# Triangular inverses in a delta-rule attention kernel: 16-by-16 blocks on VectorE, joined to 32-by-32 by TensorE

## The chip, the cores and the metric

The kernel runs on one core of one Trainium2 chip. The metric is the device time of one execution in microseconds (us), from the first to the last instruction with what lies around them; lower is better. The median of three runs of the kernel before is 1263.36 us.

## What is computed

A delta-rule attention over 4 batches, 8 heads, 768 tokens and a head dimension of 48 is followed by two dense feed-forward stages on 3072 tokens of 384 features. The reference, cut to what matters:

```python
def _attn_ref(q, k, v, beta):
    k_n = k / (np.linalg.norm(k, axis=-1, keepdims=True) + 1e-06)
    for t in range(S):
        kt, vt, bt = (k_n[:, :, t], v[:, :, t], beta[:, :, t, None])
        y[:, :, t] = np.einsum('bhd,bhde->bhe', q[:, :, t], state)
        v_old = np.einsum('bhde,bhd->bhe', state, kt)
        state = state + bt[:, :, :, None] * np.einsum('bhd,bhe->bhde', kt, vt - v_old)

def _moe_ref(x, w_in, w_out):            # 384 -> 2048 -> 384
    h = np.maximum(x @ w_in, 0.0)
    return (h * h @ w_out)

def _moe2_ref(x, w_gate, w_val, w_out):  # 384 -> 1536 -> 384
    gate = 1.0 / (1.0 + np.exp(-(x @ w_gate)))
    return (gate * (x @ w_val) @ w_out)
```

## The kernel before

**Attention by chunks.** The 768 tokens are cut into 12 chunks of 64. Inside a chunk the recurrence is solved at once: a strictly triangular 64-by-64 matrix A (k k^T times a factor for each row, tile `am`) gives the inverse of I + A, and the rest of the chunk is products with it. A unit is a pair of heads of one batch in one chunk; its head a = 0 lies on partitions 0 to 63, a = 1 on 64 to 127. A group g is two chunks, which is 32 units in four pieces j of 8; there are six groups.

**The inverse.** Of each 64-by-64 matrix the two diagonal 32-by-32 blocks are inverted by VectorE (DVE) in `invert_ops`: three transposes bring A into `xi` with one instance of a block on each partition, then `row(j)` for j = 31 down to 1 subtracts multiples of row j in `tt` (a multiply on L408 and a subtract on L415; columns in two spans, 0 to 21 and 22 to 31, where both exist), then `t_out` (L420) and `t_1` (L425) transpose back into `t64` and `t1` (which is the place of `xi`). The block between the two is made by TensorE (PE) and ScalarE (ACT): `n_piece` (L440) multiplies A's block with the one inverse, `w_piece` (L460) with the other, four pieces to a group. `t_piece`, `y_piece`, `s_piece` and `ks_piece` then use `t64`.

**The two stages.** In the first stage six passes, one for each group, run 16 iterations of the first feed-forward (`moe1_h`, L603, and `moe1_o`, L642), with weights as pairs of 12-bit parts, three products for each product of the reference. ACT squares, DVE or GpSimd (POOL) makes the low part `gl` (L628), and POOL the low parts of the weights (`ol`, `il`, L130). The attention of the next groups is spread over these passes. In the second stage (from about 800 us) only the second feed-forward is left (L849, L879).

**What sets the order.** Every engine's instructions are issued in the order in which the program writes them. Before the first pass the order is a list written by hand, `P_['start']`, in which `('d', n)` puts n products that nothing reads (`keep_warm`, L717, 512 columns each) on PE, and `('inv', w)` lets DVE take steps of an inverse of a weight w. In the passes each half of an iteration is a slot, 32 to a pass, and a table gives every piece the slot at which it is written. The steps of an inverse are in the queue `t_ops`; `invert_by` takes as many at each slot as it needs to be done at the slot `t_due`. The conversion of the raw weights (`narrow`: ACT L147, DVE L152 to L165, POOL L172) is spread over the start and the first pass.

The lines on which the change bears:

```python
tmp = [atc.tile([128, n], F32, name=f"tmp{n}") for n in (128, 224)]
spans = [(i, max(j, lo), hi) for i, (lo, hi) in enumerate(((0, CUT), (CUT, 32))) if hi > j]
ops += [(0.3 + 0.0021 * j * (32 - j), lambda j=j: row(j)) for j in range(31, 0, -1)]
ops += [(1.2, lambda: t_out(32)), (1.2, t_1)]
ops += [(1.2, lambda q=q: t_out(0, slice(32 * q, 32 * q + 32))) for q in (0, 2)]
```

Of the kernel before, what the change touches and what calls it, by code (L numbers as in the profile page):

```python
# [27 lines left out]
P_ = {'start': [('kn', 0, 1), ('kc', 0, 0), ('d', 1), ('kn', 0, 0), ('kn', 0, 2), ('kn', 0, 3), ('kc', 0, 1),  # L28
# [72 lines left out]
def kernel(  # L101
# [86 lines left out]
    # The last four blocks' places hold raw weights until it is their turn.  # L188
# [57 lines left out]
    tmp = [atc.tile([128, n], F32, name=f"tmp{n}") for n in (128, 224)]  # L246
# [4 lines left out]
    # What y's contraction takes from both sides, head a and b: tokens' rows at 0 and 64 (U; the  # L251
    # masked k q^T), d's at 64 and 0 (S; q^T).
# [68 lines left out]
    def norms(g):  # L321
        """beta / (|k| + 1e-6) and +-beta / (|k| + 1e-6)^2; one Newton step after Sqrt."""
# [45 lines left out]
    def scores_p(g, j):  # L368
        """k q^T where the token of k is the earlier one."""
# [17 lines left out]

    def invert_ops():
        """The inverses' 32 x 32 diagonal blocks: 128 instances (32 rows of a head, unit) on the
        partitions, xi [column, row], tt [column, row] of the transpose."""  # L390
# [6 lines left out]
        def t_in2(q):  # L397
            P = slice(32 * q, 32 * q + 32)
            nc.vector.transpose(out=xi[P], in_=am[P, :, 32:64].rearrange("p u c -> p c u"))

        def row(j):
            # Two spans of the columns, which do not depend on each other.
            spans = [(i, max(j, lo), hi) for i, (lo, hi) in enumerate(((0, CUT), (CUT, 32))) if hi > j]
            tv = {}
            for i, lo, hi in spans:
                n = hi - lo
                tv[i] = tmp[i][:, 0:j * n].rearrange("p (c i) -> p c i", i=n)
                nc.vector.tensor_tensor(  # L408
                    out=tv[i],
                    in0=xi[:, 0:j, j].unsqueeze(2).to_broadcast([128, j, n]),  # L410
                    in1=tt[:, j, lo:hi].unsqueeze(1).to_broadcast([128, j, n]),
                    op=ALU.mult,
                )
            for i, lo, hi in spans:
                nc.vector.tensor_tensor(  # L415
                    out=tt[:, 0:j, lo:hi], in0=tt[:, 0:j, lo:hi], in1=tv[i], op=ALU.subtract
                )
# [8 lines left out]

        ops = [(1.2, t_in), (1.2, lambda: t_in2(1)), (1.2, lambda: t_in2(3))]
        ops += [(0.3 + 0.0021 * j * (32 - j), lambda j=j: row(j)) for j in range(31, 0, -1)]
        ops += [(1.2, lambda: t_out(32)), (1.2, t_1)]
        ops += [(1.2, lambda q=q: t_out(0, slice(32 * q, 32 * q + 32))) for q in (0, 2)]  # L430
        return ops

# [62 lines left out]
    def t_piece(g, j):  # L495
        R = kv_t[g, j][:, :, HD:2 * HD]
# [31 lines left out]
    def y_piece(g, j):  # L528
# [104 lines left out]
    def moe1_o(n):  # L633
# [76 lines left out]
    def keep_warm(n, out=None):  # L710
        """Products that nothing reads, which keep the array's clock up while it waits."""
# [7 lines left out]
    with tc.manual_schedule():  # L719
# [15 lines left out]
        for g in range(1, NG):  # L735
            put_chain(g, S1 * (g - 1) + base[g])
            if g + 1 < NG:
                put_scores(g + 1, S1 * (g - 1) + base[g], S1 * g + base[g + 1])
# [4 lines left out]
        # The places of the raw weights of f, and who has them next.  # L743
        nxt = {f: f + 3 for f in range(NF1 - 7)}
        nxt.update({NF1 - 6: NF1 - 4, NF1 - 5: NF1 - 3, NF1 - 3: NF1 - 2, NF1 - 2: NF1 - 1})
        for f, t in zip(range(4, NF1), P_["cv"]):
# [165 lines left out]
def _layout(inputs):  # L912
# [8 lines left out]
    # axes: half, b2, pair, head, step, token, d  # L921
# [43 lines left out]
```

## Time and profile before

| | |
|---|---|
| runs | 1255.98, 1263.36, 1266.18 us |
| span of the profiled execution | 1259.9 us |
| busy PE, DVE, ACT, POOL | 1131.8, 749.4, 532.0, 392.3 us |
| start, until the first product of the first feed-forward | 0 to 97 us |
| first stage, first pass (17 iterations until the next pass's first `moe1_o`) | 97 to 286 us |
| second, third and fourth pass | 286 to 406, 406 to 532, 532 to 665 us |
| fifth and sixth pass | 665 to 740, 740 to 800 us |
| second stage | 800 to 1260 us |

The shares of busy time are means over stages with different limits, so the table cuts the span where a pass's `moe1_o` begins. PE counts a product in single precision (the attention's) as two instructions. The granted clock of PE has two levels, 1.2 and 2.4 GHz, shown as 0.50 and 1.00; a value between is a mean over a stretch.

### The profile page before, as it was taken

How to read it: one execution, taken by the hardware profiler on the slowest of the kernel's cores; microseconds unless marked ns; L12 is line 12 of the kernel's file. 1: busy time of each engine (PE TensorE's matmuls, PEld its weight loads, DVE VectorE, ACT ScalarE, POOL GpSimd, SP SyncE). 2: the span in 40 equal slices, each digit the busy share in tenths (PEclk: the TensorE clock that was granted, in tenths of full speed). 3: DMA queues.
4: the chain of work that ended last, by engine and by line, in shares of the span. 5: the costliest groups of instructions: out<-in, count | busy, mean ns of one | idle time of the engine just before them, and what ended most of it. 6: DMA issues, size and time to landing. Idle time of an engine off the chain costs nothing.

```text
span 1259.9 us, 24397 instructions
## 1 busy us (share of the span) xinstructions
PE 1131.8 (90%) x10040; PEld 923.1 (73%) x10040; DVE 749.4 (59%) x1416; ACT 532.0 (42%) x998; POOL 392.3 (31%) x331
## 2 busy tenths in 40 slices
PE   7675568789978997798899999999999999999997
PEld 4354456668856775586678888788888888888886
DVE  7999999996899599969954323342222222222222
ACT  3144354546544654465347668532122222222211
POOL 3444474644354345433333555200010100001000
PEclk9677679988989999899869999999999999999999
DMA  9014422602234224512313012320101010010101
GB/s 246 9 66 143 120 93 73 188 18 87 82 119 118 89 80 126 151 59 82 108 39 115 26 63 82 107 75 3 48 1 51 1 45 6 1 51 1 26 1 26
DMA packets 59552, 88.98 MB, mean 71 GB/s; under 512 B 31536, under 2 KB 39344, under 8 KB 59440
## 3 DMA queue, kind: packets, MB, share of 16 engines
q1 hardware_dynamic: 59440, 87.42, 22.9%
q8 instruction: 79, 1.29, 0.4%
q14 instruction: 33, 0.27, 0.1%
HBM read 66.16 MB, written 16.52 MB: 66 GB/s over the span
## 4 chain that ended last, share of the span: by engine, by line
PE 50%; issue 2%; DVE 2%; POOL 1%; DMA 0%; ACT 0%; DVEq 0%; POOLq 0%
PE gv L849 24%; PE o L879 12%; PE o L642 6%; PE h L603 6%; PE att L477 1%; DVE tt L415 0%; PE att L502 0%; DVE tmp L408 0%; POOL il L130 0%; PE att L536 0%; DVE pq L386 0%; PE att L350 0%; PE att L460 0%; POOL y L172 0%; PE att L440 0%
## 5 line engine op out<-in xcount | busy, mean ns | idle before, releaser
L857 DVE TENSOR_TENSOR p<-sg,gv 128x512 f32<-128x512 f32 x72 | 49.5, 688 | 284.1 <-PE gv L849 284.1
L130 POOL TENSOR_TENSOR ol<-w1r,oh 128x384 fp32r<-128x384 f32 x73 | 94.5, 1295 | 209.4 <-ACT oh L129 206.7
L642 PE MATMUL o<-gl,oh 128*128 128x512 f32 x288 | 123.7, 430 | 33.0 <-DVE gl L628 33.0
L642 PE MATMUL o<-gh,ol 128*128 128x512 f32 x288 | 122.3, 425 | 25.8 <-POOL ol L130 25.8
L619 ACT ACTIVATE gg<-h 128x512 f32<-128x512 f32 x96 | 57.4, 598 | 197.1 <-PE h L603 104.2
L130 POOL TENSOR_TENSOR xlo<-x2r,xhi 128x512 fp32r<-128x512 f32 x18 | 25.1, 1394 | 340.3 <-ACT xhi L129 340.3
L642 PE MATMUL o<-gh,oh 128*128 128x512 f32 x288 | 125.7, 436 | 0.4 <-ACT oh L129 0.4
L849 PE MATMUL gv<-xhi,w2l 128*128 128x512 f32 x432 | 123.3, 394 | 0.0
L849 PE MATMUL gv<-xhi,w2h 128*128 128x512 f32 x432 | 123.3, 394 | 0.0
L849 PE MATMUL gv<-xlo,w2h 128*128 128x512 f32 x432 | 123.2, 393 | 0.0
L855 ACT ACTIVATE sg<-gv 128x512 f32<-128x512 f32 x72 | 43.1, 599 | 181.9 <-PE gv L849 181.9
L415 DVE TENSOR_TENSOR tt<-tt,tmp 128x21 f32<-128x21 f32 (+37 forms) x312 | 116.1, 404 | 2.1
L408 DVE TENSOR_TENSOR tmp<-xi,tt 128x21 f32<-128x21 f32 (+37 forms) x312 | 111.2, 388 | 2.3
L859 ACT CAST ph<-p 128x512 fp32r<-128x512 f32 x72 | 44.7, 620 | 159.2 <-DVE p L857 159.2
L628 DVE TENSOR_TENSOR gl<-gg,gh 128x512 fp32r<-128x512 f32 x88 | 79.2, 905 | 37.3 <-ACT gg L622 37.1
L879 PE MATMUL o<-w2h,pl 128*128 128x384 f32 x288 | 97.4, 338 | 0.0
L879 PE MATMUL o<-w2h,ph 128*128 128x384 f32 x288 | 97.2, 338 | 0.0
L879 PE MATMUL o<-w2l,ph 128*128 128x384 f32 x288 | 97.1, 337 | 0.0
L642 PEld LDWEIGHTS o<-gl,oh 128*128 128x128 f32 x288 | 59.7, 207 | 50.3 <-DVE gl L628 37.4
L603 PE MATMUL h<-xhi,ih 128*128 128x512 f32 (+1 forms) x291 | 92.6, 427 | 4.0 <-ACT xhi L129 4.0
L849 PEld LDWEIGHTS gv<-xlo,w2h 128*128 128x128 f32 x432 | 81.3, 188 | 18.9
L849 PEld LDWEIGHTS gv<-xhi,w2l 128*128 128x128 f32 x432 | 81.1, 188 | 18.8
(122 smaller groups left out, 2246.6 us busy)
## 6 DMA issues: line engine op xcount, KB each, us to landing
raw<-in_w_dram SPq DMA_DIRECT2D x25, 768.0 KB, 5.0
kv<-in_kv_dram SPq DMA_DIRECT2D x24, 384.0 KB, 4.7
w1s<-in_w_dram SPq DMA_DIRECT2D x9, 768.0 KB, 4.4
w2d<-y SPq DMA_DIRECT2D x18, 384.0 KB, 2.7
t<-w2d SPq DMA_DIRECT2D x12, 576.0 KB, 3.7
kn<-in_kv_dram SPq DMA_DIRECT2D x24, 192.0 KB, 5.7
kc<-in_kq_dram SPq DMA_DIRECT2D x48, 96.0 KB, 2.8
pq<-in_kq_dram SPq DMA_DIRECT2D x48, 96.0 KB, 3.4
```

The costliest lines, as they stand in the source:

```text
L130: eng.tensor_tensor(out=dst_lo, in0=src, in1=dst_hi.bitcast(F32), op=ALU.subtract)
L408: nc.vector.tensor_tensor(out=tv[i], in0=xi[:, 0:j, j].unsqueeze(2).to_broadcast([128, j, n]), in1=tt[:, j, lo:hi].unsqueeze(1).to_broadca ...
L415: nc.vector.tensor_tensor(out=tt[:, 0:j, lo:hi], in0=tt[:, 0:j, lo:hi], in1=tv[i], op=ALU.subtract)
L603: nc.tensor.matmul(out=ps[:, cs], lhsT=w[:, kc * 128:kc * 128 + 128], rhs=x[:, kc, cs], start=(i == 0 and kc == 0), stop=(i == 2 and kc == ...
L619: nc.scalar.activation(out=gg, in_=ps, func=ACTF.Relu)
L628: (nc.gpsimd if n in P_['gp'] else nc.vector).tensor_tensor(out=gl, in0=gg, in1=gh.bitcast(F32), op=ALU.subtract)
L642: nc.tensor.matmul(out=po[m], lhsT=w[:, cs], rhs=x, start=(f == 0 and i == 0), stop=(f == NF1 - 1 and i == 2),)
L849: nc.tensor.matmul(out=ps, lhsT=w[:, kc * 128:kc * 128 + 128], rhs=x[:, kc, :], start=(i == 0 and kc == 0), stop=(i == 2 and kc == KD - 1),)
L855: nc.scalar.activation(out=sg, in_=pss[0], func=ACTF.Sigmoid)
L857: nc.vector.tensor_tensor(out=p, in0=sg, in1=pss[1], op=ALU.mult)
L859: nc.scalar.copy(out=ph, in_=p)
L879: nc.tensor.matmul(out=po2[m], lhsT=x[:, cs], rhs=w, start=(f == 0 and i == 0), stop=(f == NF2 - 1 and i == 2),)
```

## The change

VectorE inverts only the 16-by-16 blocks on the diagonal, two of each 32-by-32 instance in one instruction (`both` walks them 16 * 33 elements apart), 15 rows instead of 31. Two new functions join them on PE. `join_a` multiplies A's block between the two with the one inverse for all 32 units and 4 quadrants, on top of a constant that one product with an identity puts into PSUM. `join_b` multiplies with the other, and a third set of 64 products makes the transposed copy `t1`. ACT moves the results, and fills the left half of `t64`, which DVE's last two transposes did before. A list of constants is made once by POOL at the start. In the passes `join_a` and `join_b` stand 4 and 2 slots ahead of the chain's first slot, and the inverse is due 4 slots earlier than before. The last two steps of an inverse now wait, in program order, until the four `t_piece` of the group before have been written.

```diff
+JOIN = (4, 2)
...
-           ('kt', 1, 0), ('d', 1), ('kc', 0, 2), ('be',), ('d', 6), ('d', 2), ('sq', 0, 0), ('d', 2),
+           ('kt', 1, 0), ('cs',), ('d', 1), ('kc', 0, 2), ('be',), ('d', 6), ('d', 2), ('sq', 0, 0), ('d', 2),
...
-           ('v', 0, 3), ('d', 15), ('h', 0), ('p', 0, 0), ('d', 6), ('kt', 1, 3), ('d', 6), ('a', 1, 2),
+           ('v', 0, 3), ('d', 15), ('ja',), ('h', 0), ('p', 0, 0), ('d', 6), ('kt', 1, 3), ('d', 6), ('a', 1, 2),
...
-           ('sm', 1, 0), ('inv', 6), ('n', 0, 0), ('d', 2), ('v', 0, 0), ('n', 0, 1), ('d', 1), ('w', 0, 0),
+           ('sm', 1, 0), ('jb',), ('inv', 6), ('n', 0, 0), ('d', 2), ('v', 0, 0), ('n', 0, 1), ('d', 1), ('w', 0, 0),
...
         def row(j):
+            n = 16 - j
+            tv = tmp[:, 0:2 * j * n].rearrange("p (b c i) -> p b c i", b=2, i=n)
+            nc.vector.tensor_tensor(
+                out=tv, in0=both(xi, j, [32, j], [0, n]), in1=both(tt, 33 * j, [0, j], [1, n]), op=ALU.mult
+            )
+            t = both(tt, j, [32, j], [1, n])
+            nc.vector.tensor_tensor(out=t, in0=t, in1=tv, op=ALU.subtract)
...
+        ops += [(0.3 + 0.004 * j * (16 - j), lambda j=j: row(j)) for j in range(15, 0, -1)]
+        ops += [(2.2, t_out), (2.0, t_1)]
...
+    def join_a():
+        ps = att_ps()
+        psv = ps.rearrange("p (u c) -> p u c", u=32)
+        nc.tensor.matmul(out=ps, lhsT=ib, rhs=cb.rearrange("p u c -> p (u c)"), start=True, stop=False)
+        for u in range(32):
+            for q in range(4):
+                c = 32 * (q % 2)
+                nc.tensor.matmul(
+                    out=psv[32 * q:32 * q + 16, u, :], lhsT=am[quad(q), u, c:c + 16], rhs=t64[quad(q), u, 48:64],
+                    start=False, stop=u == 31,
+                )
+        nc.scalar.mul(out=nf[:, :, 16:32], in_=psv, mul=-1.0)
+    def join_b():
...
+                nc.tensor.matmul(
+                    out=psv[quad(q), u, :], lhsT=t1[quad(q), u, :], rhs=nf[quad(q), u, 16:32], start=True, stop=True
+                )
+        nc.scalar.copy(out=t64[:, :, 48:64], in_=psv)
...
+            for q in (0, 2):
+                nc.tensor.matmul(
+                    out=psv[quad(q), u, :], lhsT=nf[quad(q), u, :], rhs=t1[quad(q), u, 0:16], start=True, stop=True
+                )
+        for q in (0, 2):
+            nc.scalar.copy(out=t1[quad(q), :, 0:16], in_=psv[quad(q)])
+            nc.scalar.copy(out=t64[quad(q), :, 0:32], in_=t64[quad(q), :, 32:64])
...
     def invert(us):
         while t_ops and us > 0:
+            if len(t_ops) <= 2 and t_seen[0] < t_seen[1]:
+                break
...
+        put(b - JOIN[0], join_a)
+        put(b - JOIN[1], join_b)
```

**PE at the start.** The first place is PE's order ahead of `n_piece` of the first group. Before, the products of `scores_p` (L375) follow the unread ones (`idle`, L717) without a wait for the inverse:

```order
L717 LDWEIGHTS z
L717 MATMUL idle<-z 128x512
L375 MATMUL att<-pq_115,kc 64x64 x16
L717 LDWEIGHTS z
L717 MATMUL idle<-z 128x512
```

Now the first join, which reads the inverse in `t64`, stands between them (L453 is the constant, L457 the products of `join_a`, L381 is `scores_p`, L777 the unread products):

```order
L777 MATMUL idle<-z 128x512
L453 LDWEIGHTS ib
L453 MATMUL att<-cb,ib 128x512
L457 MATMUL att<-t_108,am 16x16 x128
L381 MATMUL att<-pq_117,kc 64x64 x16
L777 LDWEIGHTS z
```

What stood between L375 and `n_piece` before (64 products of attention and 48 unread ones) now stands between the two joins; further on in PE's order, directly ahead of `n_piece` (L491), comes `join_b`:

```order
L777 MATMUL idle<-z 128x512
L469 MATMUL att<-nf,xi 32x16 x128
L477 MATMUL att<-xi,nf 32x16 x64
L491 MATMUL att<-t_108,am 32x32 x16
L777 LDWEIGHTS z
```

So PE reads the first inverse one whole list of products earlier than before, and `n_piece` follows 192 new products.

**DVE at the end of an inverse.** The second place is DVE's order in the second pass, where the inverse of the fourth group ends. Before (L408 and L415 are a row's multiply and subtract, L420 and L425 the transposes back, L628 is `gl`, L386 is `scores_p`):

```order
L408 TENSOR_TENSOR tmp_111<-xi,tt 128x21
L408 TENSOR_TENSOR tmp_112<-xi,tt 128x10
L415 TENSOR_TENSOR tt<-tt,tmp_111 128x21
L415 TENSOR_TENSOR tt<-tt,tmp_112 128x10
L420 STREAM_TRANSPOSE t_108<-tt 128x32x32
L386 TENSOR_TENSOR pq_115<-att,mask 64x512 x2
L628 TENSOR_TENSOR gl<-gg,gh 128x512
L425 STREAM_TRANSPOSE xi<-tt 128x32x32
L386 TENSOR_TENSOR pq_116<-att,mask 64x512 x2
L420 STREAM_TRANSPOSE t_108<-tt 32x32x32
```

Now, at the end of the same inverse (L431 and L435 are a row, L438 and L441 the transposes, L680 is `gl`):

```order
L680 TENSOR_TENSOR gl<-gg,gh 128x512
L431 TENSOR_TENSOR tmp<-xi,tt 128x30
L435 TENSOR_TENSOR tt<-tt,tmp 128x2x15
L438 STREAM_TRANSPOSE t_108<-tt 128x32x32
L441 STREAM_TRANSPOSE xi<-tt 128x32x32
L680 TENSOR_TENSOR gl<-gg,gh 128x512
```

Each row is one pair of instructions now, and the two transposes of a quadrant (L420, 32x32x32) are gone from DVE.

**ACT in the same pass.** The third place is ACT's order where `join_b` stands; nothing stood here before between L149 (`high`) and L671 (`moe1_h`'s first activation):

```order
L149 ACTIVATE raw<-raw 128x768
L472 COPY t_108<-att 128x32x16
L481 COPY xi<-att 32x32x16
L482 COPY t_108<-t_108 32x32x32
L481 COPY xi<-att 32x32x16
L482 COPY t_108<-t_108 32x32x32
L671 ACTIVATE gg<-h 128x512
```

Five copies of a join now stand ahead of the activation on which `gl` of that iteration waits.

## Rows read from the trace of the kernel before

**Rows 1.** Busy by stretch: length, PE PEld DVE ACT POOL, clock, DMA share, GB/s.

```profile
97.00:190.00 93.00, 55.53 (x723) 43.54 (x721) 91.13 (x137) 41.25 (x78) 53.02 (x38) 0.72 0.40 121
190.00:286.00 96.00, 79.86 (x883) 63.27 (x884) 92.00 (x177) 47.58 (x91) 50.23 (x40) 0.90 0.30 91
286.00:350.00 64.00, 64.00 (x945) 51.50 (x942) 48.70 (x105) 39.73 (x79) 26.61 (x25) 0.96 0.27 86
350.00:406.00 56.00, 42.42 (x384) 32.22 (x382) 55.48 (x117) 26.22 (x51) 26.98 (x20) 0.91 0.42 123
406.00:532.00 126.00, 109.09 (x1402) 85.62 (x1396) 108.01 (x232) 67.25 (x134) 56.05 (x45) 0.93 0.35 107
532.00:665.00 133.00, 120.86 (x1550) 94.92 (x1544) 103.83 (x225) 68.38 (x139) 48.06 (x44) 0.88 0.25 82
665.00:740.00 75.00, 75.00 (x567) 61.47 (x562) 30.22 (x51) 54.21 (x104) 36.79 (x34) 1.00 0.14 47
```

**Rows 2.** PE's waits, 97 to 665: who, for whom, total us, times, longest.

```profile
PE o L642 <- DVE gl L628: 33.0, 11, 7.4
PE o L642 <- POOL ol L130: 25.1, 9, 12.2
...
PE h L603 <- ACT xhi L129: 4.0, 2, 2.3
```

**Rows 3.** Other engines' waits, 97 to 665.

```profile
ACT gg L619 <- DVE gl L628: 76.1, 13, 9.2
POOL y L172 <- DVE raw L165: 53.1, 12, 10.1
...
ACT w1s L147 <- DMA raw<-in_w_dram: 15.1, 3, 11.7
```

**Rows 4.** The page's costliest groups: busy us, mean ns, idle us before.

```profile
L415 DVE TENSOR_TENSOR tt<-tt,tmp 128x21 f32<-128x21 f32 (+37 forms) x312 | 116.1, 404 | 2.1
L408 DVE TENSOR_TENSOR tmp<-xi,tt 128x21 f32<-128x21 f32 (+37 forms) x312 | 111.2, 388 | 2.3
```

**Rows 5.** Groups kept apart by form: transposes, a product's own duration, ACT copies.

```profile
L420 DVE STREAM_TRANSPOSE t<-tt 32x1024 f32<-32x1024 f32 x12 | 26.8, 2237 | 0.2
...
L440 PE MATMUL att<-t,am 32*32 32x32 f32 x768 | 19.7, 211 | 27.8 <-DVE t L420 17.4 <-DVE pq L386 6.7 <-DVE ks L490 2.3
...
L358 ACT COPY ar<-att 128x512 f32<-128x512 f32 x4 | 2.3, 581 | 1.4 <-PE att L350 1.4
```

**Rows 6.** DVE in order of time, first inverse: start us, us, instruction.

```profile
21.08 0.21 DVE L408 TENSOR_TENSOR tmp<-xi,tt 128x31 f32<-128x31 f32 x1
...
23.27 0.30 DVE L408 TENSOR_TENSOR tmp<-xi,tt 128x135 f32<-128x135 f32 x1
...
30.20 1.53 DVE L408 TENSOR_TENSOR tmp<-xi,tt 128x40 f32<-128x40 f32 x2
```

**Rows 7.** PE in order of time, 8 to 60.

```profile
8.30 3.29 PE L350 MATMUL att<-kc 48*64 48x64 f32 x96
13.19 1.18 PE L350 MATMUL att<-kc 48*64 48x64 f32 x32 [1.60 <-DVE am L361]
...
20.12 1.15 PE L375 MATMUL att<-pq,kc 48*64 48x64 f32 x32
...
31.71 2.14 PE L375 MATMUL att<-pq,kc 48*64 48x64 f32 x32 [3.83 <-DMA pq<-in_kq_dram]
...
42.54 2.55 PE L717 MATMUL idle<-z 128*128 128x512 bf16 x11
55.76 1.06 PE L440 MATMUL att<-t,am 32*32 32x32 f32 x32 [10.68 <-DVE t L420]
```

**Rows 8.** The same products in the second pass, PE in order of time.

```profile
292.24 0.69 PE L440 MATMUL att<-t,am 32*32 32x32 f32 x32
```

**Rows 9.** Busy time by stretch at the start, columns as in Rows 1.

```profile
14.20:17.60 3.40, 3.40 (x42) 2.29 (x38) 3.25 (x4) 0.00 (x0) 0.00 (x0) 0.50 0.99 313
```

**Rows 10.** POOL's longest wait, at the start.

```profile
POOL kv L301 <- DMA kv<-in_kv_dram: 19.8, 1, 19.8
```

More of the change, by code (lines that the diff above doesn't have):

```diff
@@ L245 @@
     tt = atc.tile([128, 32, 32], F32, name="tt")
-    tmp = [atc.tile([128, n], F32, name=f"tmp{n}") for n in (128, 224)]
+    tmp = atc.tile([128, 128], F32, name="tmp")
+    nf = work.tile([128, 32, 32], F32, tag="nf", name="nf", bufs=1)
+    ib = work.tile([128, 128], BF16, tag="ib", name="ib", bufs=1)
+    cb = work.tile([128, 32, 16], BF16, tag="cb", name="cb", bufs=1)
     def att_ps():
@@ L386, in scores_p, with quad, constants, diagonal @@
                 nc.vector.tensor_tensor(out=po, in0=psv[tok(a)], in1=ma, op=ALU.mult)
+    def quad(q):
+        return slice(32 * q, 32 * q + 32)
+    def constants():
+        for t, v in ((ib, 1.0), (cb, -1.0), (nf[:, :, 0:16], 1.0)):
+            nc.gpsimd.memset(t, v)
+        def diagonal(t, pattern, base):
+            nc.gpsimd.affine_select(
+                out=t, in_=t, pattern=pattern, base=base, channel_multiplier=-1, compare_op=ALU.is_equal, fill=0.0
+            )
+        diagonal(ib, [[1, 128]], 0)
+        for q in range(4):
+            diagonal(cb[quad(q)], [[0, 32], [1, 16]], 16)
+            diagonal(nf[quad(q), :, 0:16], [[0, 32], [1, 16]], 0)
     def invert_ops():
@@ L397, in t_in2, with both @@
         def t_in2(q):
-            P = slice(32 * q, 32 * q + 32)
-            nc.vector.transpose(out=xi[P], in_=am[P, :, 32:64].rearrange("p u c -> p c u"))
+            nc.vector.transpose(out=xi[quad(q)], in_=am[quad(q), :, 32:64].rearrange("p u c -> p c u"))
+        def both(t, at, *dims):
+            return bass.AP(t.tensor, t.offset + at, [list(t.ap[0]), [16 * 33, 2], *dims])
         def row(j):
-            spans = [(i, max(j, lo), hi) for i, (lo, hi) in enumerate(((0, CUT), (CUT, 32))) if hi > j]
@@ L404, in row @@
[L404 to L417, printed above, removed]
@@ L424, in t_1, with t_out @@
+            nc.vector.tensor_tensor(out=t, in0=t, in1=tv, op=ALU.subtract)
+        def t_out():
+            nc.vector.transpose(out=t64[:, :, 32:64].rearrange("p u i -> p i u"), in_=tt.rearrange("p c i -> p i c"))
         def t_1():
             nc.vector.transpose(out=t1.rearrange("p u c -> p c u"), in_=tt)
-        ops = [(1.2, t_in), (1.2, lambda: t_in2(1)), (1.2, lambda: t_in2(3))]
-        ops += [(0.3 + 0.0021 * j * (32 - j), lambda j=j: row(j)) for j in range(31, 0, -1)]
-        ops += [(1.2, lambda: t_out(32)), (1.2, t_1)]
@@ L430, in invert_ops @@
-        ops += [(1.2, lambda q=q: t_out(0, slice(32 * q, 32 * q + 32))) for q in (0, 2)]
-        return ops
+        ops = [(2.1, t_in), (2.0, lambda: t_in2(1)), (2.0, lambda: t_in2(3))]
+        ops += [(0.3 + 0.004 * j * (16 - j), lambda j=j: row(j)) for j in range(15, 0, -1)]
+        ops += [(2.2, t_out), (2.0, t_1)]
+        return ops
+    def join_a():
+        assert not t_ops
+        ps = att_ps()
+        psv = ps.rearrange("p (u c) -> p u c", u=32)
+        nc.tensor.matmul(out=ps, lhsT=ib, rhs=cb.rearrange("p u c -> p (u c)"), start=True, stop=False)
+        for u in range(32):
+            for q in range(4):
+                c = 32 * (q % 2)
[4 more added lines that the diff above has]
+        nc.scalar.mul(out=nf[:, :, 16:32], in_=psv, mul=-1.0)
@@ new lines, in join_b @@
+    def join_b():
+        ps = att_ps()
+        psv = ps.rearrange("p (u c) -> p u c", u=32)
+        for u in range(32):
+            for q in range(4):
+                nc.tensor.matmul(
+                    out=psv[quad(q), u, :], lhsT=t1[quad(q), u, :], rhs=nf[quad(q), u, 16:32], start=True, stop=True
+                )
+        nc.scalar.copy(out=t64[:, :, 48:64], in_=psv)
+        ps = att_ps()
+        psv = ps.rearrange("p (u c) -> p u c", u=32)
+        for u in range(32):
+            for q in (0, 2):
[5 more added lines that the diff above has]
+            nc.scalar.copy(out=t64[quad(q), :, 0:32], in_=t64[quad(q), :, 32:64])
@@ L495, in t_piece @@
     def t_piece(g, j):
+        t_seen[0] += 1
         R = kv_t[g, j][:, :, HD:2 * HD]
@@ L677 @@
     t_due = [0]
+    t_seen, t_starts = [0, 0], [0]
     def invert_by(t):
@@ L684, in start_invert @@
         t_ops.extend(invert_ops())
+        t_seen[1] = 4 * (t_starts[0])
+        t_starts[0] += 1
         t_due[0] = t
@@ L737 @@
             if g + 1 < NG:
-                put_scores(g + 1, S1 * (g - 1) + base[g], S1 * g + base[g + 1])
+                put_scores(g + 1, S1 * (g - 1) + base[g], S1 * g + base[g + 1] - JOIN[0])
         for i, steps in enumerate(w2_todo):
@@ L755 @@
             be=lambda: nc.sync.dma_start(out=beta_t, in_=beta), f=fetch,
-            sq=lambda g, j: squares(g, j, True), sm=sums, no=norms, a=scores_a, st=lambda g: start_invert(0 if g == 0 else base[1]),
+            sq=lambda g, j: squares(g, j, True), sm=sums, no=norms, a=scores_a, st=lambda g: start_invert(0 if g == 0 else base[1] - JOIN[0]),
             inv=invert, d=keep_warm, h=high, p=scores_p, v=scale_v, n=n_piece, w=w_piece, sa=scale_a, b=bits, l=low, t=t_piece, y=y_piece, s=s_piece,
-            run=run, ci=conv_in, co=conv_out, x=lambda g, st: x_split(g, st, nc.gpsimd), xv=lambda g, st: x_split(g, st, nc.vector), ks=ks_piece,
+            run=run, ja=join_a, jb=join_b, cs=constants, ci=conv_in, co=conv_out, x=lambda g, st: x_split(g, st, nc.gpsimd), xv=lambda g, st: x_split(g, st, nc.vector), ks=ks_piece,
         )
```

3 lines of the change are left out of this document (removed).

## The prediction

> **What bounds the kernel now.** I read busy time by stretch first, then PE's waits, then the orders. In the second stage, and in the fifth and sixth pass, PE is busy without a break at the full clock: 75.00 us of 75, clock 1.00 [rows 1]. No inverse is left there, so the change can win nothing in them. In the first four passes PE stands idle for 37.5 + 16.1 us (97 to 286), 0 + 13.6 (286 to 406), 16.9 and 12.1: each is the length of the stretch less PE's busy time [rows 1]. That is 96.2 us. Its clock is also low in parts of them. Per stretch, (1 - clock) times busy PE gives what that costs: 15.5 + 8.0, 2.6 + 3.8, 7.6 and 14.5, in all 52.0 us. Together 148 us could be had in these passes, 77 in the first and 71 in the other three.
>
> DVE is the reason. It is busy 91.13 of 93 and 92.00 of 96 us in the first pass, and 55.48 of 56 us where the second one stalls, while between 286 and 350, at 48.70 of 64, PE never waits [rows 1]. The longest sums of PE's waits name `gl`, 33.0 us, and `ol`, 25.1 us [rows 2]. `gl` is a DVE instruction that stands behind rows of an inverse. `ol` is POOL's, but ACT, which feeds it, waits 76.1 us for `gl`, and POOL 53.1 us for DVE's part of the weights' conversion [rows 3]. Only small waits are of another kind, such as 4.0 us for `xhi` [rows 2].
>
> **What it takes from DVE.** A row's two lines cost 116.1 + 111.2 us [rows 4], 37.9 for each of six inverses, and the two transposes of a quadrant 2 x 2.24 [rows 5]. The new rows are 30 instructions of 2j(16 - j) elements, 30 to 128. Rows of that size take 0.21 to 0.30 us alone, with 0.04 between [rows 6], so 8.7 us for 30. Beside POOL's work a pair takes 1.53 us [rows 6], 0.77 each, which would make 23. I take 12, because in the passes most rows stand where POOL is half busy [rows 1]. So DVE loses about 30 us per group. From 406 to 532 that leaves 78 of its 108 us, two thirds of a stretch of 115.
>
> **What it adds to PE.** Per group 128 + 128 + 64 products, 640 instructions, and one of 512 columns. The nearest is `n_piece`, 32 by 32: 32 instructions end 0.69 us after the first begins [rows 8], the last one's own length being about 0.19 to 0.21 [rows 5]: 16 ns each. 640 of them make 10.2 us, with the constant 10.5. Below, 8 ns, if the four quadrants overlap where `n_piece` has two (5 us a group). Above, 25 ns, half way to the (3.29 - 1.18) / 64 = 33 ns of a 48 by 64 one [rows 7]. I take 16, because shape and quadrants are closest. Five groups fall into the passes, two of them into the first: 52 us on the engine that becomes the bound.
>
> The Trainium skill, TensorEngine Tiling (Array Packing), § Instruction Overhead, speaks against such small products: each has some 60 cycles of overhead, and one column costs as much as 60. At 2.4 GHz that is 25 ns an instruction, an estimate from that page, 16 us a group instead of 10.5, which would make the sum some 35 us worse. The trace does not bear it out so far: a 32 by 32 product costs half of a 48 by 64 one; for 16 columns no run here shows it.
>
> **Waits, ACT, POOL, SP.** `join_a` waits for DVE's transpose, with all of PE behind it; so did `n_piece` before, four slots later. Its copy on ACT waits for PE in turn, with the next scores' copies and raw weights behind. ACT gets per group two copies of 128x512 at 0.58 [rows 5], two of 32x512, which I price alike, and two of 32x1024, 1.1 each by twice the columns: 4.5 us, taken as nothing, since ACT is busy 67.25 of 126 us [rows 1]; without that cover 27 us in six groups. POOL's twelve constants lie in the 19.8 us which it waits at the start [rows 10]; SP's queue is unchanged.
>
> **The start** gains nothing, because of the order. The rows begin at 21.08 as before [rows 6] and end near 29.8 + 2.2 for the transpose, at 32. `join_a` stands before `scores_p`, which ran at 20.12, so PE idles until 32, then needs 4 to 7 us (16 to 27 ns; 27 is `n_piece` at 55.76, in low clock [rows 7]). Behind it queue all the products that filled the wait before, from 20.12 to 45.09 less 3.83 of waiting for a DMA: 21.1 us [rows 7]. They end at 57 to 60, `join_b` 3 to 6 us later, and `n_piece` starts at 61 to 67 instead of 55.76 [rows 7]. From there on I give back 4 us, since the unread products now stand right before `join_b` and keep the clock up, which had fallen in 10.68 us of idling (`n_piece` took 1.06 us there [rows 7], 0.69 later [rows 8]), and 1.5 us because DVE's first rows no longer stand ahead of the next group's `ks_piece`; the joins' ACT copies take 2 back. Loss 0 to 11, taken as 5.
>
> **The sum.** Of the first pass's 77 us I count three quarters, 58: DVE's conversions of weights, POOL and the DMAs stay in step there. Of the other 71 I count 85%, 60. What is left out covers DVE's transposes, ACT's copies ahead of `gl`, and the clock behind a long run of small products: after 128 of 48 by 64, with a gap of 1.60 us, it fell to 1.2 GHz from 14.20 to 17.60 [rows 7, 9]; once after each of ten joins would cost 10 x 3.4 / 2 = 17 us. So -58 - 60 + 52 + 5 = -61: 1259.9 becomes 1199 for the profiled execution. The median of the runs lies 3.5 us above that span, so **1203 us**.
>
> **Rivals.**
>
> 1. *The first pass keeps its waits.* POOL and ACT take over, with the raw weights' conversion as the chain. For it: ACT waits 15.1 us for raw weights' DMAs [rows 3], and PE 25.1 for `ol`. Against it: POOL is busy 53 of 93 us, ACT 41 [rows 1]. If three tenths of the 77 come back, not three quarters, the time is 35 us higher: 1238. Chance 0.13.
>
> 2. *Every product costs 25 ns*, as if the quadrants overlapped less than `n_piece`'s do. 640 x 9 ns = 5.8 us a group, six groups 35: 1238. Against it: 16 ns for 32 by 32. Chance 0.13; it is the result of the rule above.
>
> 3. *Four quadrants overlap*, 8 ns, nine tenths of the waits vanish, and the start loses nothing: -133 + 26 = -107, near 1156; halfway to it 1180. Chance 0.12.
>
> 4. *Slower: products in one PSUM bank wait for each other.* `join_a` adds to a bank which the constant has filled, each product is tiny, and 128 follow each other; unoverlapped, one takes 211 ns [rows 5]. Each ns above 16 costs 640 x 6 = 3.8 us: gain and loss meet at 32 ns, and at 211 the kernel would be at 1950. For it: nothing in the trace adds so many small products in one bank. Against it: `n_piece` writes 16 of them into one bank without it. Chance 0.05.
>
> 5. *No change*: rivals 1 and 2 together, 1273, or with some of rival 3, about 1255. Chance 0.07. That DVE's rows are not cut is excluded by the order.
>
> **How the numbers follow.** The forecast, 1185 to 1222, has 0.50. The range, 1172 to 1242, holds it, 0.23 of rivals 1 and 2, and 0.08 of rival 3, the part nearer to the forecast: 0.81. The bounds of the products (5 to 16 us a group: -28 to +35) and of the start (-5 to +6) are in it. One per cent, 12.6 us, is about what a measurement of this kernel can tell from no change: below 1250.7 lie the forecast, rival 3, and nearly all of 1 and 2, 0.86; within 1% 0.08; slower 0.06.
>
> **What would show it.** Right: PE's waits for `gl` from 286 to 665 under 10 us in all; DVE busy near two thirds there; the new rows 8 to 20 us a group; 640 new instructions at 13 to 20 ns; the first four passes near 152, 113, 116 and 121 us instead of 189, 120, 126 and 133; the first `n_piece` at 61 to 67 us. Wrong: joins over 25 ns an instruction; PE waiting for `ol` as long as before with DVE idle; clock falls after each join; or `n_piece` before 55.

## The result and the profile after

The changed kernel takes 1269.35 us (median of 10 runs, 1265.18 to 1271.81), the kernel before 1261.8 in the same session (10 runs). The ratio is 1.0056, 95% interval 1.0034 to 1.0077: within 1%, and if anything slower. The forecast was 1203, with a range from 1172 to 1242. The profiled span is 1268.9 us.

The stages as the prediction cuts them. The start ends with the first product of `h`, and a pass with the next one's first product of `o`. The third column is an experiment that leaves the joins' small products out.

| us | before | after | after, without products |
|---|---|---|---|
| start | 97.3 | 111.8 | 86.4 |
| first pass | 189.1 | 187.8 | 165.4 |
| second, third, fourth pass | 119.6, 126.3, 133.1 | 122.8, 121.6, 130.5 | 102.7, 104.0, 109.7 |
| span | 1259.9 | 1268.9 | 1162.7 |

The same stages after: length, busy PE (instructions), granted clock, DMA share, GB/s.

```profile
0.00:111.80 111.80, 78.63 (x1838) 0.79 0.34 92
111.80:299.60 187.80, 153.93 (x2892) 0.83 0.37 109
299.60:422.40 122.80, 112.86 (x1961) 0.93 0.34 103
422.40:544.00 121.60, 114.48 (x2058) 0.94 0.36 107
544.00:674.50 130.50, 121.88 (x2182) 0.92 0.27 87
```

PE's waits after, from 0 to 740: who, for whom, total us, times, longest. They answer to [rows 2].

```profile
PE att L457 <- issue: 16.0, 6, 4.8
PE att L469 <- issue: 13.2, 6, 3.9
PE att L457 <- DVE t L438: 11.8, 1, 11.8
PE o L694 <- DVE gl L680: 8.4, 5, 3.4
PE att L477 <- issue: 8.1, 6, 2.1
...
PE o L694 <- POOL ol L132: 1.4, 1, 1.4
```

The waits that the change was expected to end did end: `gl` fell from 33.0 to 8.4 us and `ol` from 25.1 to 1.4. In their place stand 37.3 us put down to "issue", that is, to nothing that the profile shows, on three new lines: the products of the joins (L457, L469, L477), with six waits each in six groups. Not every wait put down to "issue" is new: the longest one, 4.96 us on L381 in the first pass, stands in the kernel before too (5.24), and no packet of PE's instructions (theory A below) falls into it.

DVE behaves as expected (busy in one stretch, columns as in [rows 1], then the groups that answer to [rows 4]):

```profile
406.00:532.00 126.00, 118.23 (x2089) 96.15 (x2085) 76.49 (x140) 73.80 (x141) 48.61 (x43) 0.91 0.34 101
```

```profile
L435 DVE TENSOR_TENSOR tt<-tt,tmp 128x30 f32<-128x30 f32 (+7 forms) x90 | 37.9, 421 | 3.1
L431 DVE TENSOR_TENSOR tmp<-xi,tt 128x30 f32<-128x30 f32 (+7 forms) x90 | 33.0, 367 | 2.7
```

The rows take 70.9 / 6 = 11.8 us a group. DVE is busy 76.49 of 126 us where it was 108.01 [rows 1].

Now a join, PE in order of time: start us, us, instruction, count, and in brackets the idle time before it.

```profile
385.80 0.39 PE L453 MATMUL att<-cb,ib 128*128 128x512 bf16 x1
386.12 2.22 PE L457 MATMUL att<-t,am 32*16 32x16 f32 x249
393.15 0.24 PE L457 MATMUL att<-t,am 32*16 32x16 f32 x7 [4.81 <-issue]
393.32 1.65 PE L655 MATMUL h<-xhi,ih 128*128 128x512 f32 x3
...
400.63 1.83 PE L469 MATMUL att<-nf,xi 32*32 32x16 f32 x197
404.39 0.98 PE L469 MATMUL att<-nf,xi 32*32 32x16 f32 x58 [1.93 <-issue]
...
407.84 1.78 PE L477 MATMUL att<-xi,nf 32*32 32x16 f32 x59 [0.65 <-issue]
409.56 1.65 PE L655 MATMUL h<-xhi,ih 128*128 128x512 f32 x3
```

249 instructions (the matmuls of the trace, their weight loads counted apart) in 2.22 us are under 9 ns each, half of what I had priced. Then PE stops for 4.81 us with only seven left. The two parts take 393.32 - 385.80 = 7.5 and 409.56 - 400.63 = 8.9 us; over the five groups in the passes the two parts together take 14.5 to 17.0 us, 15.7 in the mean, 24 ns an instruction. Behind a stop the products of `h` are slow: three take 1.65 us here and at most 0.97 in the fifth pass. The clock in these stretches:

```profile
384.00:388.00 4.00, 4.00 (x240) 1.00 0.76 219
388.00:393.30 5.30, 0.49 (x48) 0.74 1.08 312
393.30:400.00 6.70, 6.70 (x39) 0.69 0.19 39
```

While the 240 small products run the clock is full. It falls in the stop and stays low for part of the 6.70 us behind it.

### The profile page after: what moved, and what is told of

Its sections match the earlier page's. It is cut to its first block, busy times and chain, and to the rows that moved or that the text cites. A ratio compares the mean times of both kernels' runs of the same rounds, so it can differ in the third digit from the quotient of the medians.

```text
span 1268.9 us, 31676 instructions
## 1 busy us (share of the span) xinstructions
PE 1168.3 (92%) x13871; PEld 966.1 (76%) x13886; DVE 605.8 (48%) x960; ACT 558.3 (44%) x1034; POOL 383.4 (30%) x343
## 3 DMA queue, kind: packets, MB, share of 16 engines
q8 instruction: 109, 1.79, 0.6%
## 4 chain that ended last, share of the span: by engine, by line
PE 51%; DVE 2%; issue 1%; ACT 0%; POOL 0%; DVEq 0%
PE gv L909 24%; PE o L939 12%; PE o L694 7%; PE h L655 6%; DVE tt L435 1%; PE att L528 1%; DVE tmp L431 0%; PE att L554 0%; PE att L588 0%; DVE xi L422 0%; PE att L381 0%; PE att L356 0%; PE att L477 0%; DVE us L578 0%; DVE gl L680 0%
## 5 line engine op out<-in xcount | busy, mean ns | idle before, releaser
L132 POOL TENSOR_TENSOR ol<-w1r,oh 128x384 fp32r<-128x384 f32 x73 | 81.9, 1121 | 242.9 <-ACT oh L131 242.8
L132 POOL TENSOR_TENSOR xlo<-x2r,xhi 128x512 fp32r<-128x512 f32 x18 | 25.1, 1394 | 340.2 <-ACT xhi L131 340.2
L694 PE MATMUL o<-gl,oh 128*128 128x512 f32 x288 | 118.2, 410 | 8.4 <-DVE gl L680 8.4
L671 ACT ACTIVATE gg<-h 128x512 f32<-128x512 f32 x96 | 57.4, 598 | 148.3 <-PE h L655 129.0
L694 PE MATMUL o<-gh,ol 128*128 128x512 f32 x288 | 118.2, 411 | 2.1 <-POOL ol L132 2.1
L680 DVE TENSOR_TENSOR gl<-gg,gh 128x512 fp32r<-128x512 f32 x88 | 80.6, 922 | 37.4 <-ACT gg L674 37.2
L939 PE MATMUL o<-w2h,ph 128*128 128x384 f32 x288 | 97.2, 338 | 0.0
L909 PEld LDWEIGHTS gv<-xhi,w2h 128*128 128x128 f32 x432 | 80.3, 188 | 12.8
L655 PE MATMUL h<-xhi,il 128*128 128x512 f32 (+1 forms) x291 | 87.1, 410 | 0.0
L132 POOL TENSOR_TENSOR il<-w1r,ih 128x384 fp32r<-128x384 f32 x72 | 84.6, 1175 | 1.4 <-ACT ih L131 1.4
```

What stands on the lines that cost most here:

```text
L655: nc.tensor.matmul(out=ps[:, cs], lhsT=w[:, kc * 128:kc * 128 + 128], rhs=x[:, kc, cs], start=(i == 0 and kc == 0), stop=(i == 2 and kc == ...
L671: nc.scalar.activation(out=gg, in_=ps, func=ACTF.Relu)
L680: (nc.gpsimd if n in P_['gp'] else nc.vector).tensor_tensor(out=gl, in0=gg, in1=gh.bitcast(F32), op=ALU.subtract)
L694: nc.tensor.matmul(out=po[m], lhsT=w[:, cs], rhs=x, start=(f == 0 and i == 0), stop=(f == NF1 - 1 and i == 2),)
L909: nc.tensor.matmul(out=ps, lhsT=w[:, kc * 128:kc * 128 + 128], rhs=x[:, kc, :], start=(i == 0 and kc == 0), stop=(i == 2 and kc == KD - 1),)
L939: nc.tensor.matmul(out=po2[m], lhsT=x[:, cs], rhs=w, start=(f == 0 and i == 0), stop=(f == NF2 - 1 and i == 2),)
```

## The theories

**A, supply of instructions.** The page counts PE's instructions and the packets that bring instructions in:

```profile
PE 1168.3 (92%) x13871; PEld 966.1 (76%) x13886; DVE 605.8 (48%) x960; ACT 558.3 (44%) x1034; POOL 383.4 (30%) x343
...
q8 instruction: 109, 1.79, 0.6%
```

27757 instructions of PE, weight loads included, in 109 packets are 255 to a packet, that is 128 products with their weight loads. A group's 640 products are five packets. Theory A: in a run of products of 8 ns PE empties what was brought in ahead, and then waits for each packet; the clock falls in that wait.

**B, the product.** A product of this kind costs about 24 ns, in whatever place it stands (the second rival of the prediction, and the fourth in a mild form).

**C, the chain.** The joins wait for DVE's transposes and ACT's copies; what PE shows as a wait is that chain.

## The experiments

### Runs of unread products in the fifth pass

In the fifth pass PE waits for nothing [rows 1], so what is added there is seen bare. Each call in the code shows as two products in the trace, each with its weight load; the numbers here count products. The wide ones take 64 rows of `t64` and 64 columns of `am`.

```diff
+    def burst(n, wide=False):
...
+        for i in range(n // 8):
+            for q in range(4):
...
+                    nc.tensor.matmul(
+                        out=psv[quad(q), i % 32, :], lhsT=t1[quad(q), i % 32, :], rhs=nf[quad(q), i % 32, 16:32],
+                        start=True, stop=True,
+                    )
...
+        for t, n in ((148, 128), (150, 256), (152, 640)) + tuple((t, 64) for t in range(156, 164)):
+            put(t, burst, n)
+        put(146, burst, 256, True)
```

> Added to the changed kernel: unread products in the fifth pass, where PE waits for nothing: one run of 256 instructions of 64 columns, then runs of 128, 256 and 640 instructions of 32x32 by 16, then eight of 64, a slot apart. Theory A: the run of 128 takes 1.1 to 1.5 us without a gap; 256 take 2.2 to 4 us; 640 take 12 to 15 us, with three or four gaps of about 2 us, one per 128 instructions, a packet of 16384 bytes ahead of each, and the clock falls in it; the 256 wide ones, 33 ns each, show no gap; the eight of 64 take 0.55 us each without one. Theory B: all small ones cost the same, 24 ns each, in every run. If the small products alone lower the clock: it falls in the eight runs of 64 or in that of 128 as well.

PE in order of time (L490 is the wide run, L495 the small ones):

```profile
713.27 7.68 PE L490 MATMUL att<-am,t 64*64 64x64 f32 x256
...
725.20 1.26 PE L495 MATMUL att<-nf,xi 32*32 32x16 f32 x128
...
730.70 1.78 PE L495 MATMUL att<-nf,xi 32*32 32x16 f32 x190
734.69 0.74 PE L495 MATMUL att<-nf,xi 32*32 32x16 f32 x66 [2.22 <-issue]
...
741.29 1.63 PE L495 MATMUL att<-nf,xi 32*32 32x16 f32 x172
745.28 1.26 PE L495 MATMUL att<-nf,xi 32*32 32x16 f32 x128 [2.36 <-issue]
749.02 1.90 PE L495 MATMUL att<-nf,xi 32*32 32x16 f32 x128 [2.48 <-issue]
...
756.79 1.36 PE L495 MATMUL att<-nf,xi 32*32 32x16 f32 x84 [1.84 <-issue]
...
769.03 0.73 PE L495 MATMUL att<-nf,xi 32*32 32x16 f32 x64
```

The clock in some of these stretches (columns: length, busy PE, clock, DMA share, GB/s), then the packets between 740.5 and 758.1 (count, MB, share):

```profile
724.50:727.00 2.50, 2.50 (x135) 1.00 0.03 7
740.50:758.10 17.60, 8.79 (x645) 0.67 0.02 5
758.10:762.00 3.90, 3.90 (x11) 0.50 0.00 0
768.00:790.00 22.00, 22.00 (x572) 1.00 0.01 3
```

```profile
q8 instruction: 5, 0.08, 2.3%
```

A is shown and B falls. The same product costs about 9 ns in runs of 64 and 128, without a stop. In a run of 256 PE stops once, after 190. In the run of 640 it stops after 172 and then after each 128, and five packets come in. In the trace the packets of the four stops begin at 742.64, 746.43, 750.25 and 754.10 us and take 1.2 to 1.4 us, and PE goes on 1.3 to 1.5 us after each has ended. From 745.28 to 756.79 three stretches of 128 take 11.5 us, 3.8 each, so a long run costs some 30 ns an instruction; the 640 take 16.8 us and the 256 take 4.7, both longer than expected. The 256 wide ones, at 30 ns each, never stop. Small products don't lower the clock by themselves: it stays at 1.00 over the run of 128, over the runs of 64, and over the 263 which the changed kernel's start has without a stop (63.10 to 65.40 us). Behind the run of 256, with its one stop, it is 0.55 from 736 to 739 us, and behind the run of 640 0.50, 1.2 GHz, over 3.90 us. The kernel as a whole took 1314.06 us (one run), with 1792 unread instructions added.

### The joins without their products

Left out: all 640 small products of a group; the product with the constant fills the three banks instead. Copies and transposes stay, and the inverse is not computed. The same edit stands at the two places of `join_b`.

```diff
-        nc.tensor.matmul(out=ps, lhsT=ib, rhs=cb.rearrange("p u c -> p (u c)"), start=True, stop=False)
-        for u in range(32):
-            for q in range(4):
-                c = 32 * (q % 2)
-                nc.tensor.matmul(
...
+        nc.tensor.matmul(out=ps, lhsT=ib, rhs=cb.rearrange("p u c -> p (u c)"), start=True, stop=True)
```

> Left out: all 640 small products of a group; the constant's product fills the three banks instead, and all copies and transposes stay, so the inverse is not computed. Theories A and B: what the relief of VectorE is worth without the joins: five groups of about 15.6 us in the passes, about 10 us at the start, and the clock that falls behind the joins, some 20 us: 1150 to 1175 us. Theory C: the copies and their waits stay, so 1230 us or more.

1163.95 us, 0.9208 of before (0.9147 to 0.9268). By stage, and PE's longest sum of waits from 86.4 to 568:

```profile
0.00:86.40 86.40, 66.92 (x1201) 0.88 0.47 118
86.40:251.80 165.40, 130.33 (x1616) 0.89 0.42 122
251.80:354.50 102.70, 100.14 (x1321) 1.00 0.41 120
354.50:458.50 104.00, 102.66 (x1417) 1.00 0.42 126
458.50:568.20 109.70, 107.27 (x1546) 1.00 0.32 103
```

```profile
PE o L679 <- POOL ol L132: 10.5, 5, 7.5
```

C falls, though not by this run alone: the copies and transposes are in place and 106 us go away, but the product with the constant reads neither `t64` nor `nf`, so PE's waits for DVE and ACT at the joins are left out too. In the changed kernel itself the only long wait of that kind on the joins' lines is the 11.8 us of L457 at the start; in the passes none of their waits names DVE or ACT. This run splits the change in two. Relieving DVE is worth 97.2 us of span (1259.9 to 1162.7), the products cost 106.2 (1162.7 to 1268.9), the wait at the start included. In the passes two to four PE stands idle for only 6.3 us in all, and the clock is at 1.00 throughout.

### The joins in pieces

Four pieces of 8 units for each join, in different slots, at first close to the blocks that read them; 640 instructions as before.

```diff
-        put(b - JOIN[0], join_a)
-        put(b - JOIN[1], join_b)
+ 'ja': [[-4, -4, -3, -3], [-7, -6, -3, -1]],
+ 'jb': [[-2, -2, -1, 1], [-4, -2, 0, 2]],
...
+        for j in range(4):
+            put(b + P_["ja"][g > 1][j], join_piece, join_a, j)
+            put(b + P_["jb"][g > 1][j], join_piece, join_b, j)
```

> The joins of the five groups made in the passes are cut into four pieces of 8 units, each with its own constant, bank and copies, and put into different slots; the products are the same 640 per group, and the start keeps its two runs. Theory A (instruction supply): in a run of small products PE empties what was fetched ahead, waits about 2 us for the next packet, and the clock falls in that wait. With 32 to 96 products at a time the waits put down to 'issue' on the joins' lines fall from 37 us to under 12 us (what is left is the start), products cost 8 to 16 ns, the low clock behind the joins goes too: 1225 to 1240 us. Theory B (the products themselves cost about 24 ns, wherever they stand): no gain, 1262 to 1275 us. Theory C (the joins are held by the chain DVE, PE, ACT, PE): four short chains per group wait more than two long ones, 1270 to 1290 us.

1253.68 us, 0.9918 of before (0.9888 to 0.9949). The sign is A's, the size is about half of what I expected. PE's waits from 285.2 to 661.1:

```profile
PE att L502 <- ACT t L479: 2.8, 2, 1.4
PE att L502 <- issue: 2.7, 1, 2.7
```

The first pass, columns as in the stages above:

```profile
112.40:285.20 172.80, 142.31 (x2802) 0.89 0.40 120
```

The gain is all in the first pass, 172.8 us where it was 187.8. The passes two to four took 118.1, 124.6 and 133.2 us, together no less than before, though their "issue" waits fell from 19.9 to some 8 us. There the waits for packets left the joins and came back, smaller, on the small products that follow close behind (L502, L539, 2.0 us), and the pieces' copies on ACT were now read at once. In the first pass a piece also waited 8.2 us for DVE, since I had made it due too early.

So the pieces were put farther away, into slots of their own, and the last 128 instructions of a group (L477), which only compute the transpose of what is there, were given back to DVE. The lists hold the slots of the four pieces, ahead of a group's base, for group 1, for group 2 and for the later ones:

```diff
-            nc.scalar.copy(out=t1[quad(q), s, 0:16], in_=psv[quad(q)])
+            nc.vector.transpose(out=t1[quad(q), s], in_=t64[quad(q), s, 32:64])
+ 'ja': [[], [-4, -4, -3, -3], [-6, -5, -4, -3], [-10, -9, -8, -7]],
+ 'jb': [[], [-2, -2, -1, 1], [-4, -2, -1, 1], [-6, -4, -3, -2]],
```

> As e1_pieces, with three differences: the last 128 of the 640 instructions of a group are replaced by VectorE's transposes of the two blocks (eight of 32x256 a group); from the third group on the pieces stand in eight slots of their own, six to ten slots ahead of the blocks that read them, and VectorE's part is due earlier; in the first pass the second group's first piece comes one slot later, since e1_pieces waited 8 us for VectorE there. The start is that of the changed kernel. If e1_pieces kept its waits because its pieces still stood beside others of 32 instructions and their copies were read at once: the waits for 'issue' from 285 to 661 us (8.3 us there) fall under 3, those for ACT's copy under 2, the passes two to four come to 108 to 116, 110 to 118 and 116 to 124 us: 1220 to 1235 us in all. If the products' cost does not depend on the supply of instructions any more: 1248 us or more, no better than e1_pieces.

1225.18 us, 0.973 of before (0.9698 to 0.9763). The passes two and four, and PE's longest sum of waits in them:

```profile
276.50:391.00 114.50, 107.99 (x1832) 0.97 0.37 109
...
507.90:627.30 119.40, 114.54 (x2056) 0.99 0.29 94
```

```profile
PE att L462 <- DVE t L440: 10.1, 2, 5.6
```

"Issue" has come down from 19.9 us in these passes to 0.6, and the clock from 0.92 to 0.94 up to 0.97 to 0.99. Against the kernel without products a group now costs 9.7 to 12.9 us in these passes, not 17.6 to 20.8. This run changes three things at once, and a group has 512 small products here, not 640: how much of the 28 us from the run before is the slots and how much the 128 instructions was not taken apart.

### The start

POOL makes the identity alone, ACT the other constants from it once the norms are done; the first join goes behind two of the four pieces of score products, the second follows behind the other two, and 16 unread products are gone (three and 38 in the expectation are miscounts).

```diff
-           ('v', 0, 3), ('d', 15), ('ja',), ('h', 0), ('p', 0, 0), ('d', 6), ('kt', 1, 3), ('d', 6), ('a', 1, 2),
+           ('v', 0, 3), ('d', 15), ('h', 0), ('p', 0, 0), ('d', 6), ('kt', 1, 3), ('d', 6), ('a', 1, 2),
-           ('sq', 1, 2), ('a', 1, 1), ('inv', 2), ('sq', 1, 3), ('p', 0, 3), ('v', 0, 2), ('d', 4),
+           ('sq', 1, 2), ('a', 1, 1), ('inv', 2), ('sq', 1, 3), ('p', 0, 3), ('v', 0, 2), ('d', 12),
-           ('p', 0, 1), ('d', 8), ('d', 7), ('d', 6), ('p', 0, 2), ('a', 1, 3), ('d', 6), ('d', 5),
-           ('sm', 1, 0), ('jb',), ('inv', 6), ('n', 0, 0), ('d', 2), ('v', 0, 0), ('n', 0, 1), ('d', 1), ('w', 0, 0),
+           ('ja',), ('p', 0, 1), ('d', 4), ('p', 0, 2), ('jb',), ('a', 1, 3), ('d', 4),
```

> Only the start is changed: POOL makes the identity alone and ACT copies the other constants from it once the norms are done, and the first join stands behind three of the score products rather than ahead of them, the second four products' worth of copies later, with 38 fewer unread products. If the start's loss of 14 us comes from the order and from POOL's constants beside DVE's small instructions: the first row at 21 to 22 us instead of 24.65, the first n_piece at 45 to 50 instead of 70.7, the first product of the first pass at 88 to 98 instead of 111.8, 1245 to 1255 us. If the weights' conversion or a DMA holds the first pass back whatever attention does: the first pass begins at 105 us or later, 1262 us or more.

1254.01 us, 0.9941 of before (0.9914 to 0.9967). The first pass begins at 99.0 us instead of 111.8, so 12.8 of the 14.5 us lost at the start came from the order, the constants and the unread products together, and a first pass that begins earlier does not give it back (186.6 us, 187.8 in the changed kernel). The first `n_piece` stood at 61.05, though, not at 45 to 50: the rows now ran beside POOL's masks and the join began at 37.99, and the joins at the start still stopped for packets (1.75, 2.12 and 0.92 us).

The constants alone, with the order left as it was:

> The changed kernel with one thing of e4_start alone: POOL makes the identity only, ACT the other constants later. If POOL's ten other instructions beside VectorE's small ones cost the start its first 3.6 us: the norms' instructions of 128x32 take 0.18 us each again instead of up to 1.01, the first row begins at 21 to 22 us, not at 24.65, and all comes 2 to 4 us earlier: 1264 to 1268 us. If they did not: the first row at 24 us or later, and no gain.

DVE in order of time, of the changed kernel and then of this one:

```profile
12.40 0.79 DVE L337 TENSOR_SCALAR n<-n 128x32 f32<-128x32 f32 x1
...
24.65 0.20 DVE L431 TENSOR_TENSOR tmp<-xi,tt 128x30 f32<-128x30 f32 x1
```

```profile
11.53 0.18 DVE L337 TENSOR_SCALAR n<-n 128x32 f32<-128x32 f32 x1
...
22.10 0.20 DVE L433 TENSOR_TENSOR tmp<-xi,tt 128x30 f32<-128x30 f32 x1
```

POOL's constants ran from 6.72 to 14.8 us, beside DVE's norms. Its TENSOR_SCALAR and TENSOR_TENSOR instructions of 128x32 took up to 0.79 us beside them and 0.18 to 0.19 without. The 1.01 us of the expectation belong to the last one, at 14.87 us, when POOL had gone on to filling `tt` (14.88, 0.95 us); the next instruction of DVE did not start later for it. The first row begins 2.55 us earlier, the first pass 2.4 (109.4). In time that is 1268.46 us (one run), too little to tell.

### Both together, and a last step

> e5_spread with the start of e4_start, its joins too in pieces, between the score products. If the two are independent, e5_spread's time less 13 to 20 us: 1203 to 1222 us, faster than both kernels. If the start's gain is eaten in the first pass, which waits for the weights' conversion: e5_spread's time less 0 to 6 us.

```diff
+           ('ja', 0), ('ja', 1), ('p', 0, 1), ('ja', 2), ('d', 2), ('jb', 0), ('ja', 3), ('p', 0, 2), ('jb', 1), ('a', 1, 3),
+           ('jb', 2), ('d', 2), ('sm', 1, 0), ('jb', 3), ('inv', 6), ('n', 0, 0), ('d', 2), ('v', 0, 0), ('n', 0, 1), ('d', 1), ('w', 0, 0),
```

1210.39 us, 0.9613 of before (0.9575 to 0.9651): faster than both kernels. The start ends at 93.3 us. Its gain against the spread joins alone, 105.8 - 93.3 = 12.5 us, arrives whole: 13.7 in the spans. The last step made the pieces of the last two groups due two slots later, where PE had waited for DVE.

```diff
- 'ja': [[], [-4, -4, -3, -3], [-6, -5, -4, -3], [-10, -9, -8, -7]],
- 'jb': [[], [-2, -2, -1, 1], [-4, -2, -1, 1], [-6, -4, -3, -2]],
+ 'ja': [[], [-4, -4, -3, -3], [-6, -5, -4, -3], [-10, -9, -8, -7], [-8, -7, -6, -4]],
+ 'jb': [[], [-2, -2, -1, 1], [-4, -2, -1, 1], [-6, -4, -3, -2], [-5, -3, -2, 0]],
```

> e6_spread_start with the pieces of the last two groups two slots later (first at 8 instead of 10 slots ahead), because PE waited there 5.6 and 4.4 us for VectorE's transpose. If that wait was only VectorE's due time: it falls under 1 us, and 1198 to 1207 us. If PE then waits in the next blocks for ACT's copies or for packets of instructions again, as in e1_pieces: 1208 us or more.

A miss: 1212.23 us, 0.9644 (0.9602 to 0.9686), not to be told from the version before it. One of the two waits went (10.1 us in all before, 4.3 after); 2.6 us more of waits for `gl` and 1.0 of "issue" came, and the other wait, 4.3 us, stayed. Why DVE is late there I did not find out.

## Why the prediction was wrong, by its own steps

The run without products lets each term of the sum be measured, by span:

| term | predicted | measured |
|---|---|---|
| relief of DVE, first pass | -58 | 165.4 - 189.1 = -23.7 |
| relief of DVE, passes two to four | -60 | 316.4 - 379.0 = -62.6 |
| joins of five groups in the passes | +52 | 562.7 - 481.8 = +80.9 |
| start | +5 | 111.8 - 97.3 = +14.5 |
| sum | -61 | +9 |

The first pass is off by 34 us, the joins by 29, the start by 9.5; only the second term held.

**What bounds the kernel.** Right in passes two to four: 62.6 of the 71 us come back, 88% where I counted 85, with the clock's part: without the products it is at 1.00 there. Right too in the rows (11.8 us a group, taken as 12), in DVE's busy share (near two thirds) and in the waits for `gl`.

**The first pass: the term that was mis-sized most.** "Of the first pass's 77 us I count three quarters" failed. Without any product on PE 23.7 of 77 come back, three tenths, which is the first rival's figure. PE waits there for `ol` 10.5 us, as I had written for that rival, but its waits that name DVE add up to more, 14.0, and DVE is still busy 145.61 of 165.4 us. So DVE, even relieved, still holds PE up there, and not POOL and ACT alone. The busy share of POOL and ACT, which I held against the rival, cannot rule out a chain through all of them. Which wait ends last there no run took apart.

**The joins: the failed step.** "16 ns, because shape and quadrants are closest" was wrong both ways. One product is cheaper: four quadrants overlap, at 8 to 9 ns in a row, the third rival's price. The Trainium skill, TensorEngine Tiling (Array Packing), § Instruction Overhead, with its 60 cycles, by estimate 25 ns at 2.4 GHz, does not hold for products that take turns over four quadrants; the 8 to 9 ns are below it. But 640 of them cost 24 ns each in the place where they stand, the second rival's price by another cause: PE stops for packets of its instructions, and the clock falls behind the stops. I asked what one product takes on the array and never what a run of them takes on the way to it. The count was to be had: 640 products are 1280 instructions, and the page of the kernel before also has a line for the packets of instructions. How fast they come, no row of before showed.

The joins' 80.9 us are made up so, as an estimate. The "issue" waits of the joins in the passes are 37.3 less the start's 1.9 and 2.1, so 33. The lost clock, (1 - clock) times busy PE over the four passes, is 50.7 us after and 14.3 in the kernel without products: 36 more. The rest, 12, is less than five times 640 products at 8.4 ns (27 us), since some of them fill waits in the first pass. If all of the lost clock is due to the stops, each microsecond that PE stood without instructions cost about another through the clock; no run separates the two. My allowance for the clock behind the joins, 17 us within the recovery, was of the right kind and half the size.

**The start: mis-sized.** The join stood where I put it in time (36.11 instead of 32) but for POOL's constants, which I had costed at nothing because POOL was idle; the work that they delay is DVE's: its first row came 3.6 us later than in the kernel before, and without the constants 2.55 of it came back.

```profile
36.11 1.49 PE L457 MATMUL att<-t,am 32*16 32x16 f32 x156 [11.76 <-DVE t L438]
...
67.63 3.23 PE L477 MATMUL att<-xi,nf 32*32 32x16 f32 x115 [2.10 <-issue]
```

Behind the join stand 112 products of attention by the code's calls, 64 of them `scores_p`, and the 48 unread ones. They ended at 63.07, where `join_b` begins, later than the 57 to 60 expected by about as much. `join_b` and its copies then took 7.6 us, not 3 to 6, with a stop of 2.10. The 5.5 us that I gave back did not come: from the first `n_piece` (70.65) to the first pass it took 41.1 us, 41.5 before.

**The rivals.** What happened is the fifth, "rivals 1 and 2 together, 1273", at a chance of 0.07. Its two terms of 35 us are near the 34 and 29 measured. But the joins' price came from the supply of instructions, not from the array, so that its time was nearly met is in part luck. The fourth, products in one bank that wait for each other, is excluded by the 8 to 9 ns in a bank.

## What to carry to other kernels

Price a run of small instructions twice: by what one takes on the engine, and by how fast instructions reach the engine, in packets of some 255. Where a block of work is cut into hundreds of small products, spread them between long ones, pieces of 64 here, and look for waits put down to nothing on the lines behind them too, with a packet of instructions ahead of their end. And a relief of one engine is worth what the run without the added work shows: leave the new work out once before trusting either term of the sum, and mind which waits go with it.

## What the runs showed of the hardware

- PE's instructions come in packets of some 255 (1.79 MB in 109). In a run of products of 9 ns PE stopped first after 118 to 263 of them and then, where the run went on, after each 128. The Trainium skill, Runtime: NRT & Kernel Launch, § Instruction fetch mechanics, has the block of 256 instructions, and the count here agrees; it also says that the fetch is hidden because instructions issue more slowly than they are brought in, and for these products the trace shows otherwise: 1.84 to 2.48 us a packet in the run of 640.
- The joins' two longest stops, 4.81 us (388.34 to 393.15, shown above) and 3.91 us (line below), stand where the DMA engines are busy with data (length, busy PE, clock, DMA share, GB/s, of the changed kernel); over the run of 640 with its ordinary stops the share is 0.02. In the trace the packets of the two long stops take no longer than others, 0.96 and 0.94 us, but begin 2.6 and 1.7 us after PE has stopped. That the data's packets delay the instructions' was not tried.

```profile
143.80:147.70 3.90, 0.00 (x1) 0.63 0.97 330
```

- Products of 32x32 by 16 that take turns over four quadrants (L469) start every 8.4 to 8.5 ns at 2.4 GHz in the joins and every 13.5 to 14.3 ns at 1.2 GHz; those that use two quadrants (L477) every 16 and 27 ns. Those of `join_a` (L457), with 16 columns of weights, start every 8.5 ns at 1.2 GHz too (36.11 to 37.60 us, clock 0.50).
- DVE's TENSOR_SCALAR and TENSOR_TENSOR instructions of 128x32 took 0.18 to 0.19 us alone and up to 0.79 us beside POOL's constants of 0.83 us.
